# A q stage with one reciprocal for each token tile, and three high-half casts moved from VectorE to ScalarE

## The chip, the cores and the metric

The kernel runs on one core of a Trainium2 chip. The metric is the device time of one execution in microseconds (us). The engines of the core are named as the profile names them: PE (TensorE matmul), PEld (its weight loads), DVE (VectorE), ACT (ScalarE), POOL (GpSimd) and SP (SyncE, which here only issues transfers). Each engine works through its own queue in order: an instruction that waits holds back everything behind it on the same engine.

## What is computed

Random-feature attention over q, k, v (4 batches, 8 heads, 576 tokens, head size 64, 128 features), then a two-matrix layer with a softplus between, then a second layer whose two products are multiplied. All of it is float32:

```python
proj = np.einsum('bhsd,md->bhsm', x, omega)
sq = np.sum(x * x, axis=-1, keepdims=True) / 2.0
h = proj - sq
h = h - np.max(h, axis=-1, keepdims=True)
return np.exp(h) / np.sqrt(m)          # phi
...
q_p, k_p = (phi(q_s), phi(k_s))
kv = np.einsum('bhsm,bhsd->bhmd', k_p, v)
z = np.sum(k_p, axis=2)
num = np.einsum('bhsm,bhmd->bhsd', q_p, kv)
den = np.einsum('bhsm,bhm->bhs', q_p, z)[..., None] + 1e-06
return (num / den).astype(np.float32)
...
g = softplus(x @ w_in);  y = g @ w_out          # first layer
return (((y @ w1) * (y @ w2)) @ w3) @ w_out2    # second layer
```

The change touches the division `num / den`, and the preparation of q for the projection on omega.

## The kernel before

A float32 product is made of three matmuls of operands that were split into a high half (`hi`, rounded) and a low half (`lo` = value minus `hi`): hi*hi, lo*hi, hi*lo (L96). The k stage comes first, then the **q stage**, then the two layers, which use fast (Strassen-like) products with sums of operands (`s1` to `s4`).

The q stage walks over 18 tiles of 128 tokens; a tile has two units of four heads. In turn t of its loop the code emits, in this order: for odd t the numerators of tile t-3; `q_turn` of tile t-2 (eight transposes on PE at L409, whose result ACT copies to `qpt` at L411); `q_feat` of tile t (24 projection matmuls, the maxima `nmax` on DVE at L349, the exponentials on ACT at L354, eight for a tile, half a tile behind); `split_q` of tile t+2 and the next load of q; `x_turn` of tile t-4 (four transposes at L439, the copy `xs` on DVE at L442 or on ACT at L444, and a transfer of it to `xd`); for even t the numerators of tile t-3. `XS_V` lists the tiles whose `xs` DVE copies: 0, 1, 7, 10, 12, 14.

`split_q` makes the halves of q. For tiles 0 to 14 DVE casts the high half (L297, `qt`) and POOL subtracts the low half (L298). Tiles 15, 16 and 17 are split ahead, in turns 9, 10 and 10 (`EARLY`), into slots of the pool `X0` (`qth`, `qtl`); there DVE does both.

`numerators` calls `q_num` for each unit: matmuls against `kv` (a 65th column gives the denominator), then on DVE an add of a small constant (L426, `den`), a reciprocal (L427) and a multiplication into `xt` (L430).

While the q stage still runs, the operands of the first layer's fast product are built from `xd`: loads `xq` on SP (L455, two buffers), casts of high halves on ACT (L469: `xa11h`, `xs1h` and so on), sums `s` (L462) and low halves (L472: `xa11l`, `xs1l` and so on) on DVE. After the last tile comes the layer itself, whose sums of products are made on DVE at L517. A scheduler places every instruction in its engine's queue when the program is built, from its own estimates of durations; a changed instruction can therefore move others too. `FILL` puts the first matmuls of the first layer between the last tiles of the q stage.

Of the kernel before, what the change touches and what calls it, by code (L numbers as in the profile page):

```python
# [19 lines left out]
F32 = mybir.dt.float32  # L20
# [4 lines left out]
ALU = mybir.AluOpType  # L25
AX = mybir.AxisListType

B, H, S, D = 4, 8, 576, 64
M = 128
NT = B * S  # L30
# [41 lines left out]
def body(ctx: ExitStack, tc: tile.TileContext, q, k, k_rest, v, v_rest, om_t, w_in, w_out, w12, w3, wo, out):  # L72
    nc = tc.nc
    cp = ctx.enter_context(tc.tile_pool(name="cp", bufs=1))
    sm = ctx.enter_context(tc.tile_pool(name="sm", bufs=1))
    M_ = ctx.enter_context(tc.tile_pool(name="M_", bufs=14))
# [6 lines left out]
    def ps():  # L83
        return ps_.tile([128, 512], F32, tag="ps", name="ps")
# [10 lines left out]
    def matmul(o, a, b, start, stop, **kw):  # L95
        nc.tensor.matmul(out=o, lhsT=a, rhs=b, start=start, stop=stop, **kw)  # L96
# [177 lines left out]
    def pair(name, bufs):  # L274
        n = small.get(name, (None, 1))[1]
        if n:
            small[name] = sm.tile([128, 2, 4], F32, tag=name, bufs=bufs, name=name), 0
        else:
            small[name] = small[name][0], 1
        return small[name][0][:, 1 - bool(n)]  # L280
# [6 lines left out]
    def xslot(pool, n, dt, name):  # L287
        return pools[pool].tile([128, n], dt, tag="x", name=name)

    kt, vt, kps, kpr, kvs, qts, kacc, raw = {}, {}, {}, {}, {}, {}, {}, {}  # L290
# [2 lines left out]
    def lined(pool, n, **kw):  # L293
        return pool.tile([128, -(-n // LINE) * LINE], F32, **kw)[:, :n]

    def split(hi, lo, f, low=None):
        nc.vector.tensor_copy(out=hi, in_=f)  # L297
        (low or nc.gpsimd).tensor_tensor(out=lo, in0=f, in1=hi.bitcast(F32), op=ALU.subtract)  # L298

    def load_k(i):  # L300
# [8 lines left out]
    def split_k(i):  # L309
        if 0 < i < 2 * B:  # L310
            kt[i] = kt[i - KBUF] if i > KBUF else [K_.tile([128, 2, 512], FR, name=f"kt{i}{x}") for x in "hl"]
            n = 128 if i == 1 else 512
            for o in range(0, 512, n):
                split(*[x[:, :, o:o + n] for x in (*kt[i], raw[i])], nc.gpsimd if i == 1 else nc.vector)
# [12 lines left out]
    def split_q(t):  # L327
        if t >= NT // 128 - len(EARLY):
            free["X0"] -= 2
            qt = [xslot("X0", 512, FR, f"qt{x}") for x in "hl"]  # L330
            split(*qt, raw[t], nc.vector)
        else:
            if len(qbuf) < QBUF:
                qbuf.append(Q_.tile([128, 2, 512], FR, name=f"qt{len(qbuf)}"))
            qt = [qbuf[t % QBUF][:, x, :] for x in range(2)]
            split(*qt, raw[t])
        qts[t] = [x.rearrange("p (c t) -> p c t", c=4) for x in qt]
# [37 lines left out]
    def matmul_half(o, a, b, start, stop):  # L375
        for c in range(0, a.shape[-1], HALF):
            matmul(o[c:c + HALF], a[:, c:c + HALF], b, start, stop, skip_group_check=True)
# [11 lines left out]
        nc.scalar.copy(out=kvs[b][:, 4 * g:4 * g + 4, :], in_=acc)  # L389

    qp, qpt, xt = {}, {}, {}

    def q_feat(u):
        t, g = divmod(u, 2)
        p = project(lambda p: [x[:, 2 * g + p, :] for x in qts[t]])
        if g and t >= NT // 128 - len(EARLY):
            free["X0"] += 2

        def exps():
            qp[u] = M_.tile([128, 4, M], F32, tag="m", name="qp")  # L400
            features(*p, qp[u])

        waiting.append(exps)
        flush(QLAG)
# [5 lines left out]
        qpt[u] = M_.tile([128, 4, 128], F32, tag="m", name="qpt")  # L410
        nc.scalar.copy(out=qpt[u], in_=tp.rearrange("p (h t) -> p h t", h=4))  # L411

    def q_num(u):
        t, g = divmod(u, 2)
        nm = ps()
        nm = nm[:, 0:4 * (D + 1)].rearrange("p (h d) -> p h d", h=4)
        lo, hi = 128 * t, 128 * t + 128
        for h in range(4):
            a = lo
            while a < hi:  # L420
                b = a // S
                e = min(hi, (b + 1) * S)
                matmul_half(nm[a - lo:e - lo, h, :], qpt[u][:, h, a - lo:e - lo], kvs[b][:, 4 * g + h, :], True, True)
                a = e
        den = pair("den", 3)[:, :, None]
        nc.vector.tensor_scalar(out=den, in0=nm[:, :, D:D + 1], scalar1=1e-6 * M, scalar2=None, op0=ALU.add)  # L426
        nc.vector.reciprocal(out=den, in_=den)  # L427
        if g == 0:
            xt[t] = M_.tile([128, H, D], F32, tag="m", name="xt")
        nc.vector.tensor_tensor(  # L430
            out=xt[t][:, 4 * g:4 * g + 4, :], in0=nm[:, :, 0:D],
            in1=den.to_broadcast([128, 4, D]), op=ALU.mult,
        )

    def x_turn(t):
        tp = ps()
# [291 lines left out]
    for i in range(2 * B):  # L728
        if i == B:
            queue += job_ops(win[:1])  # L730
        for t in range(KT):
            k_feat(i, t)
            step(JOB_K)
            if t == 0:
                load_k(i + 4)
            if t == 0 and i >= PRE:
                split_k(i + 2)
            if t == KT - 1 and i:
                kv_sum(i - 1)
                load_v(i + 2)  # L740
            if i == 2 * B - 1 and t < 2:
                split_q(t)
        if i % 4 == 0:
            for g in range(2):
                k_feat_rest(i // 2 + g)
        if i >= 2 * B - 3:
            load_q()
# [3 lines left out]
    nt = NT // 128  # L751
    begun = None

    def fill():
# [3 lines left out]
            x = Up1(0, 0, UP_RATES["Up1"][0])  # L758
            begun = x, x.begin_parts()
        next(begun[1], None)  # L760

    def numerators(t):
        if 0 <= t < nt:
            for g in range(2):
                q_num(2 * t + g)

    for t in range(nt + XLAG):
        if t % 2:
            numerators(t - NLAG)
        for g in range(2):  # L770
            if 0 <= t - TLAG < nt:
                q_turn(2 * (t - TLAG) + g)
        for g in range(2):
            if t < nt:
                q_feat(2 * t + g)
            else:
                flush(0)
            step(JOB_Q[0 in xo])
        for x in [nt - len(EARLY) + n for n, at in enumerate(EARLY) if at == t] + [t + 2] * (t + 2 < nt - len(EARLY)):
            split_q(x)  # L780
            load_q()
        if t == 1:
            kv_sum(2 * B - 1)
            kstack.close()
            pools["X0"] = ctx.enter_context(tc.tile_pool(name="X0", bufs=28, side="right", reuse_waits="tile"))
        if t >= XLAG:
            x_turn(t - XLAG)
            for c in range(2):
                if t - XLAG == 2 * N // 128 * (c + 1) - 1:
                    xo[c], ops = operands(c, xd, "X0")  # L790
                    queue += ops
        if not t % 2:
            numerators(t - NLAG)
        if t in FILL:
            fill()
# [426 lines left out]
```

## Time and profile before

| | |
|---|---|
| median of 3 runs | 811.22 us (810.95 to 811.86) |
| profiled execution | 813.02 us, its span 810.9 us |
| PE busy | 804.0 us, 99% of the span |
| DVE busy | 602.3 us, 74% |
| ACT busy | 441.2 us, 54% |
| q stage in the span | about 51 to 135 us |

The profiled execution is 1.8 us above the median of the runs, and 2.1 us longer than its own span. In a timeline row the first number is the start in us from the start of the span, the second how long it lasted from the first start to the last end, and `x8` the number of instructions in the row; the bracket at its end is the idle time of the engine just before, and what ended it. In a row of a group the numbers are the busy time in us, the mean duration in ns, and the idle time just before the group's instructions.

### The profile page before, as it was taken

Reading aid. Unit: us, or ns where it says so; the run is one execution under the profiler, and the core shown is the slowest. Engines: PE = TensorE matmul, PEld = TensorE weight load, DVE = VectorE, ACT = ScalarE, POOL = GpSimd, SP = SyncE. Lnnn points to the kernel's source line nnn. Section 1 sums busy time; section 2 is a strip of 40 time slices with the busy share of each in tenths; the row PEclk is TensorE's granted clock in tenths of the full one; section 3 lists DMA queues with packets and bytes.
Section 4 is the critical chain, followed back from the end, with each engine's and each line's share of the span. In section 5 each row is a group of like instructions: output and inputs, shape, how many; then the busy total and the mean of one; then the engine's idle time right before and its main releaser. Section 6 shows DMA issues by size and latency. Waiting matters only on the chain.

```text
span 810.9 us, 14465 instructions
## 1 busy us (share of the span) xinstructions
PE 804.0 (99%) x5462; PEld 752.4 (93%) x5462; DVE 602.3 (74%) x1022; ACT 441.2 (54%) x859; POOL 26.5 (3%) x29
## 2 busy tenths in 40 slices
PE   9999999999999999999999999999999999999998
PEld 8999999999999998888888889999999998889998
DVE  6999999878765676754569633897988876888861
ACT  6999998557445676646456432424335123674330
POOL 3033300000000000000000000000000000000000
PEclk9999999999999999999999999999999999999999
DMA  9833635656535558688994642365656556353212
GB/s 288 327 100 87 201 107 172 210 205 214 195 133 195 191 193 259 214 258 293 335 304 148 208 127 79 133 217 186 209 174 214 188 180 237 111 170 122 73 65 78
DMA packets 75861, 150.04 MB, mean 185 GB/s; under 512 B 7184, under 2 KB 44688, under 8 KB 75792
## 3 DMA queue, kind: packets, MB, share of 16 engines
q1 hardware_dynamic: 64016, 101.55, 38.1%
q10 hardware_dynamic: 11776, 47.57, 17.4%
q8 instruction: 43, 0.70, 0.4%
q14 instruction: 26, 0.21, 0.1%
HBM read 98.24 MB, written 50.86 MB: 184 GB/s over the span
## 4 chain that ended last, share of the span: by engine, by line
PE 92%; DVE 4%; DMA 2%; issue 1%; ACT 0%; POOL 0%; ACTq 0%; POOLq 0%
PE ps L96 90%; DMA xq<-xd 1%; PE ps L409 1%; DVE nmax L349 1%; DVE xt L430 1%; DVE s L462 1%; PE ps L439 0%; DVE c L517 0%; DMA rawq<-in_q 0%; DVE u L517 0%; DVE xa22l L472 0%; DVE xa12l L472 0%; DVE qt L297 0%; DVE qtl L298 0%; DVE tlo L191 0%
## 5 line engine op out<-in xcount | busy, mean ns | idle before, releaser
L96 PE MATMUL ps<-dhi,lo 128*128 128x512 f32 x256 | 99.6, 389 | 0.0
L96 PE MATMUL ps<-dlo,hi 128*128 128x512 f32 x256 | 99.6, 389 | 0.0
L96 PE MATMUL ps<-dhi,hi 128*128 128x512 f32 x256 | 99.4, 389 | 0.0
L642 DVE TENSOR_TENSOR dlo<-dn,dhi 128x512 fp32r<-128x512 f32 x64 | 43.8, 689 | 39.1 <-ACT dhi L641 23.0
L517 DVE TENSOR_TENSOR c<-ps,u 128x384 f32<-128x384 f32 x144 | 71.5, 550 | 0.8
L517 DVE TENSOR_TENSOR u<-ps,p 128x384 f32<-128x384 f32 x48 | 26.7, 556 | 53.9 <-PE ps L96 52.3
L524 ACT COPY p<-ps 128x384 f32<-128x384 f32 x48 | 23.0, 480 | 75.8 <-PE ps L96 57.3
L641 ACT CAST dhi<-dn 128x512 fp32r<-128x512 f32 x64 | 39.4, 619 | 45.2 <-DVE dlo L642 25.7
L142 DVE SCALAR_TENSOR_TENSOR f<-raw,f 128x1024 int32<-128x1024 f32 (+2 forms) x43 | 45.5, 1058 | 20.3 <-ACT raw L139 18.8
L557 ACT ACTIVATE c<-c 128x384 f32<-128x384 f32 x72 | 35.1, 524 | 46.8 <-DVE c L517 43.0
L96 PEld LDWEIGHTS ps<-dlo,hi 128*128 128x128 f32 x256 | 48.1, 188 | 10.0
L96 PEld LDWEIGHTS ps<-dhi,hi 128*128 128x128 f32 x256 | 48.1, 188 | 10.0
L96 PEld LDWEIGHTS ps<-dhi,lo 128*128 128x128 f32 x256 | 48.1, 188 | 9.8
L138 ACT ACTIVATE f<-raw,bias 128x1024 f32<-128x1024 int16 (+2 forms) x43 | 46.3, 1084 | 18.9 <-DMA raw<-in_w 9.3
L349 DVE TENSOR_REDUCE nmax<-ps 128x4 f32<-128x512 f32 x72 | 47.0, 683 | 6.2 <-PE ps L96 6.0
L139 ACT ACTIVATE raw<-raw,bias 128x1024 f32<-128x1024 int16 (+2 forms) x43 | 46.3, 1082 | 0.6
L148 DVE SCALAR_TENSOR_TENSOR f<-raw,f 128x1024 int32<-128x1024 int32 (+2 forms) x43 | 45.0, 1046 | 0.6
L354 ACT ACTIVATE qp<-ps,nmax 128x128 f32<-128x128 f32 x144 | 42.2, 457 | 2.4 <-DVE nmax L349 2.4
L354 ACT ACTIVATE kp<-ps,nmax 128x128 f32<-128x128 f32 x128 | 35.5, 460 | 6.0 <-DVE nmax L349 5.9
L96 PE MATMUL ps<-xs1h,thi 128*128 128x384 f32 x96 | 32.4, 337 | 0.2 <-DVE c L517 0.2
L96 PE MATMUL ps<-xs2h,thi 128*128 128x384 f32 x96 | 32.3, 336 | 0.0
L96 PE MATMUL ps<-xs2h,tlo 128*128 128x384 f32 x96 | 32.2, 335 | 0.0
(257 smaller groups left out, 2339.4 us busy)
## 6 DMA issues: line engine op xcount, KB each, us to landing
dn<-gd SPq DMA_DIRECT2D x64, 256.0 KB, 4.0
raw<-in_w ACTq DMA_DIRECT2D x16, 1023.8 KB, 5.8
gd<-c SPq DMA_DIRECT2D x80, 192.0 KB, 2.7
pd<-c SPq DMA_DIRECT2D x48, 192.0 KB, 2.7
raw<-in_w_out ACTq DMA_DIRECT2D x10, 767.8 KB, 4.6
raw<-in_w_in ACTq DMA_DIRECT2D x6, 1023.8 KB, 5.1
rawq<-in_q SPq DMA_DIRECT2D x18, 256.0 KB, 3.1
xd<-xs SPq DMA_DIRECT2D x18, 256.0 KB, 3.3
```

The costliest lines, as they stand in the source:

```text
L96: nc.tensor.matmul(out=o, lhsT=a, rhs=b, start=start, stop=stop, **kw)
L138: nc.scalar.activation(out=self.f, in_=top, func=AF.Relu, scale=TOP, bias=bias[:, 0:1])
L139: nc.scalar.activation(out=self.words(1, F32, 2), in_=top, func=AF.Identity, scale=TOP, bias=bias[:, 1:2])
L142: nc.vector.scalar_tensor_tensor(out=self.f.bitcast(I32), in0=self.words(1, F32, 2), scalar=-2.0 ** 31, in1=self.f, op0=ALU.max, op1=ALU.min)
L148: nc.vector.scalar_tensor_tensor(out=fi, in0=self.words(0, I32, 2), scalar=13, in1=fi, op0=ALU.logical_shift_right, op1=ALU.bitwise_or,)
L349: nc.vector.tensor_reduce(out=nmax, in_=pj, axis=AX.X, op=ALU.max, negate=True)
L354: nc.scalar.activation(out=dst[:, h, :], in_=pj[:, h, :], func=AF.Exp, bias=nmax[:, h:h + 1])
L517: nc.vector.tensor_tensor(out=z, in0=bank, in1=y, op=ALU.add)
L524: nc.scalar.copy(out=p6, in_=b1)
L557: nc.scalar.activation(out=dst, in_=src, func=AF.Softplus)
L641: nc.scalar.copy(out=hi, in_=got[m])
L642: nc.vector.tensor_tensor(out=lo, in0=got.pop(m), in1=hi.bitcast(F32), op=ALU.subtract)
```

## The change

Two things are edited. `split` takes the operation that makes the high half as an argument, and for tiles 15 to 17 that is now a copy on ACT; the low half of these tiles stays on DVE. And `q_num` is folded into `numerators`: the matmuls of both units come first, their two denominators go into one tile of 128 x 2 x 4, one reciprocal of 128 x 8 follows, then the two multiplications. There are 18 reciprocals where there were 36.

```diff
-    def split(hi, lo, f, low=None):
-        nc.vector.tensor_copy(out=hi, in_=f)
+    def split(hi, lo, f, low=None, high=nc.vector.tensor_copy):
+        high(out=hi, in_=f)
         (low or nc.gpsimd).tensor_tensor(out=lo, in0=f, in1=hi.bitcast(F32), op=ALU.subtract)
...
-            split(*qt, raw[t], nc.vector)
+            split(*qt, raw[t], nc.vector, nc.scalar.copy)
...
-    def q_num(u):
-        t, g = divmod(u, 2)
-        nm = ps()
...
-        den = pair("den", 3)[:, :, None]
-        nc.vector.tensor_scalar(out=den, in0=nm[:, :, D:D + 1], scalar1=1e-6 * M, scalar2=None, op0=ALU.add)
+    def numerators(t):
+        if not 0 <= t < nt:
+            return
+        nms = []
...
+        for g in range(2):
+            nm = ps()[:, 0:4 * (D + 1)].rearrange("p (h d) -> p h d", h=4)
...
+            nms.append(nm)
+        den = sm.tile([128, 2, 4, 1], F32, tag="den", bufs=3, name="den")
+        for g in range(2):
+            nc.vector.tensor_scalar(out=den[:, g], in0=nms[g][:, :, D:D + 1], scalar1=1e-6 * M, scalar2=None, op0=ALU.add)
         nc.vector.reciprocal(out=den, in_=den)
...
+        for g in range(2):
+            nc.vector.tensor_tensor(
+                out=xt[t][:, 4 * g:4 * g + 4, :], in0=nms[g][:, :, 0:D],
+                in1=den[:, g].to_broadcast([128, 4, D]), op=ALU.mult,
+            )
```

Line numbers after the edit are higher: the copy `xs` on ACT is L449 (before L444), the cast of an operand L474 (L469), the add of `den` L431 (L426), the reciprocal L432 (L427), the multiplication into `xt` L435 (L430), the sum `s` L467 (L462), the low half of an operand L477 (L472), `qpt` L412 (L411).

The scheduler places other instructions of the q stage anew as well. On ACT, before, in the stretch from about 101 us:

```order
L469 CAST xs3h<-s_1911 128x768
L444 COPY xs<-ps 128x512
L411 COPY qpt<-ps 128x512 x2
L354 ACTIVATE qp<-ps,nmax 128x128 x8
L444 COPY xs<-ps 128x512
L411 COPY qpt<-ps 128x512 x2
L354 ACTIVATE qp<-ps,nmax 128x128 x8
L469 CAST xs1h<-s_2020 128x768
```

In this order two copies `xs` are each followed by the `qpt` of their turn, and the cast `xs1h` comes last. The same stretch of ACT after:

```order
L474 CAST xs3h<-s_1902 128x768
L449 COPY xs<-ps 128x512
L474 CAST xs1h<-s_2009 128x768
L449 COPY xs<-ps 128x512
L412 COPY qpt<-ps 128x512 x2
L354 ACTIVATE qp<-ps,nmax 128x128 x8
L412 COPY qpt<-ps 128x512 x2
L354 ACTIVATE qp<-ps,nmax 128x128 x8
```

The cast `xs1h` and the second copy `xs` now stand ahead of the first copies `qpt`.

On DVE, before, at the end of the q stage, from the last copy `xs` that DVE makes (tile 14) to the last tile's two multiplications into `xt`:

```order
L442 COPY xs<-ps 128x512
L426 TENSOR_SCALAR den<-ps 128x4 x2
...
L472 TENSOR_TENSOR xa11l<-xq,xa11h 128x768
L430 TENSOR_TENSOR xt<-ps,den 128x256
L462 TENSOR_TENSOR s_2539<-xq 128x768
L426 TENSOR_SCALAR den<-ps 128x4
L472 TENSOR_TENSOR xs3l<-s_2492,xs3h 128x768
L427 RECIPROCAL den<-den 128x4
L426 TENSOR_SCALAR den<-ps 128x4
L430 TENSOR_TENSOR xt<-ps,den 128x256
```

In this order the first `xt` of the last tile (the last row) stands behind three operations on operands, `xa11l`, `s_2539` and `xs3l`. The same stretch of DVE after:

```order
L447 COPY xs<-ps 128x512
...
L467 TENSOR_TENSOR s_2475<-xq 128x768
...
L477 TENSOR_TENSOR xa11l<-xq,xa11h 128x768
...
L467 TENSOR_TENSOR s_2521<-xq 128x768
L435 TENSOR_TENSOR xt<-ps,den 128x256 x2
L477 TENSOR_TENSOR xs3l<-s_2475,xs3h 128x768
...
L467 TENSOR_TENSOR s_2524<-s_2521,xq 128x768
...
L477 TENSOR_TENSOR xs1l<-s_2521,xs1h 128x768
L432 RECIPROCAL den<-den 128x8
L477 TENSOR_TENSOR xs2l<-s_2524,xs2h 128x768
L435 TENSOR_TENSOR xt<-ps,den 128x256 x2
```

Now seven operations of 128x768 stand between that copy and the `xt` of the last tile; the first of them, `s_2475`, stood ahead of the copy before, as `s_2492`.

A third move on ACT has one row: the cast `thi` (L187), which stood behind the copies `qpt` of the two turns from 62 us on, stands ahead of them after. The new casts `qth` stand on ACT behind copies `xs`, two together and one by itself.

## Rows read from the trace of the kernel before

**Rows 1.** The page: busy time of the engines, and the chain by engine.

```profile
PE 804.0 (99%) x5462; PEld 752.4 (93%) x5462; DVE 602.3 (74%) x1022; ACT 441.2 (54%) x859; POOL 26.5 (3%) x29
...
PE 92%; DVE 4%; DMA 2%; issue 1%; ACT 0%; POOL 0%; ACTq 0%; POOLq 0%
```

**Rows 2.** Busy time of each engine in stretches of 20 us.

```profile
core 0: us, PE busy (x) PEld busy (x) DVE busy (x) ACT busy (x) POOL busy (x), PEclk, DMA share, GB/s
...
80.00:100.00 20.00, 19.22 (x281) 18.13 (x280) 19.27 (x49) 17.61 (x54) 7.12 (x5) 1.00 0.64 192
100.00:120.00 20.00, 19.20 (x282) 18.14 (x277) 18.82 (x54) 20.00 (x60) 0.00 (x0) 1.00 0.38 116
```

**Rows 3.** Groups of instructions by line and shape, 55 to 140 us.

```profile
L427 DVE RECIPROCAL den<-den 128x4 f32<-128x4 f32 x36 | 5.8, 168 | 0.1
...
L297 DVE CAST qth<-rawq 128x512 fp32r<-128x512 f32 x3 | 2.3, 776 | 1.0 <-DMA rawq<-in_q 1.0
...
L187 ACT CAST thi<-t 128x1024 fp32r<-128x1024 f32 x1 | 1.1, 1150 | 0.0
```

**Rows 4.** The page: the costliest groups, one cast on ACT.

```profile
L641 ACT CAST dhi<-dn 128x512 fp32r<-128x512 f32 x64 | 39.4, 619 | 45.2 <-DVE dlo L642 25.7
```

**Rows 5.** Timeline of PE, 84 to 95 us.

```profile
84.48 0.66 PE L409 MATMUL ps<-ident,qp 128*128 128x128 f32 x4
...
86.58 0.36 PE L96 MATMUL ps<-omh,qt 128*128 128x256 f32 x1 [0.41 <-DVE den L426]
...
93.37 1.09 PE L409 MATMUL ps<-ident,qp 128*128 128x128 f32 x8
94.22 0.36 PE L96 MATMUL ps<-omh,qt 128*128 128x256 f32 x1
```

**Rows 6.** Timelines of DVE and POOL, 81 to 88 us.

```profile
82.11 1.50 DVE L297 CAST qth<-rawq 128x512 fp32r<-128x512 f32 x1
...
86.35 0.17 DVE L427 RECIPROCAL den<-den 128x4 f32<-128x4 f32 x1
86.43 0.13 DVE L426 TENSOR_SCALAR den<-ps 128x4 f32<-128x4 f32 x1
...
87.52 0.40 DVE L297 CAST qth<-rawq 128x512 fp32r<-128x512 f32 x1
...
81.73 1.60 POOL L298 TENSOR_TENSOR qt<-rawq,qt 128x512 fp32r<-128x512 f32 x1 [2.89 <-DVE qt L297]
```

**Rows 7.** Timeline of PE, 101 to 104 us.

```profile
101.00 0.66 PE L409 MATMUL ps<-ident,qp 128*128 128x128 f32 x4
...
103.11 0.39 PE L96 MATMUL ps<-omh,qt 128*128 128x256 f32 x1 [0.55 <-ACT xs L444]
```

**Rows 8.** Timeline of ACT, 101 to 104 us.

```profile
101.68 0.90 ACT L469 CAST xs3h<-s 128x768 fp32r<-128x768 f32 x1
102.40 0.66 ACT L444 COPY xs<-ps 128x512 f32<-128x512 f32 x1
102.88 1.16 ACT L411 COPY qpt<-ps 128x512 f32<-128x512 f32 x2
```

**Rows 9.** Timeline of DVE at the end of the q stage.

```profile
123.63 0.95 DVE L472 TENSOR_TENSOR xs4l<-s,xs4h 128x768 fp32r<-128x768 f32 x1
124.50 0.68 DVE L442 COPY xs<-ps 128x512 f32<-128x512 f32 x1
125.10 0.22 DVE L426 TENSOR_SCALAR den<-ps 128x4 f32<-128x4 f32 x2
...
128.70 0.96 DVE L462 TENSOR_TENSOR s<-xq 128x768 f32<-128x768 f32 x1 [0.64 <-DMA xq<-xd]
...
130.72 0.42 DVE L430 TENSOR_TENSOR xt<-ps,den 128x256 f32<-128x256 f32 x1
```

**Rows 10.** Timeline of PE: the last tile's `xt` turned, and a later wait.

```profile
131.29 0.41 PE L439 MATMUL ps<-ident,xt 128*128 128x128 f32 x2 [0.28 <-DVE den L427]
...
149.89 0.44 PE L96 MATMUL ps<-xs1h,thi 128*128 128x384 f32 x1 [0.24 <-DVE c L517]
```

**Rows 11.** The chain of waits in order of time, 140 to 148 us.

```profile
140.84 7.08 DMA xq<-xd
...
147.94 0.96 DVE s L462
```

More of the change, by code (lines that the diff above doesn't have):

```diff
@@ L391, in body @@
     qp, qpt, xt = {}, {}, {}
+    nt = NT // 128
     def q_feat(u):
@@ L411, in q_turn @@
         nc.scalar.copy(out=qpt[u], in_=tp.rearrange("p (h t) -> p h t", h=4))
-    def q_num(u):
-        t, g = divmod(u, 2)
-        nm = ps()
-        nm = nm[:, 0:4 * (D + 1)].rearrange("p (h d) -> p h d", h=4)
+    def numerators(t):
+        if not 0 <= t < nt:
+            return
+        nms = []
         lo, hi = 128 * t, 128 * t + 128
[L418 to L424, printed above, removed]
-        den = pair("den", 3)[:, :, None]
-        nc.vector.tensor_scalar(out=den, in0=nm[:, :, D:D + 1], scalar1=1e-6 * M, scalar2=None, op0=ALU.add)
-        nc.vector.reciprocal(out=den, in_=den)
[L428 to L433, printed above, removed]
+        for g in range(2):
+            nm = ps()[:, 0:4 * (D + 1)].rearrange("p (h d) -> p h d", h=4)
+            for h in range(4):
+                a = lo
+                while a < hi:
+                    b = a // S
+                    e = min(hi, (b + 1) * S)
+                    matmul_half(nm[a - lo:e - lo, h, :], qpt[2 * t + g][:, h, a - lo:e - lo], kvs[b][:, 4 * g + h, :], True, True)
+                    a = e
+            nms.append(nm)
+        den = sm.tile([128, 2, 4, 1], F32, tag="den", bufs=3, name="den")
+        for g in range(2):
+            nc.vector.tensor_scalar(out=den[:, g], in0=nms[g][:, :, D:D + 1], scalar1=1e-6 * M, scalar2=None, op0=ALU.add)
+        nc.vector.reciprocal(out=den, in_=den)
+        xt[t] = M_.tile([128, H, D], F32, tag="m", name="xt")
+        for g in range(2):
[3 more added lines that the diff above has]
+            )
     def x_turn(t):
@@ L760, in fill @@
         next(begun[1], None)
[L762 to L765, printed above, removed]
     for t in range(nt + XLAG):
```

## The prediction

> **What bounds the kernel now.** I read the busy times first: PE works 99% of the span, and 92% of the chain of waits is PE [rows 1]. What other engines do counts only where PE waits for them. DVE and ACT are nearly as full as PE where the change acts: of 20 us, DVE is busy 19.27 and then 18.82, ACT 17.61 and then 20.00 [rows 2]. So work taken from DVE can help there, and work given to ACT lands on an engine without room. PE's granted clock is 1.00 in these stretches, its upper level (2.4 GHz) [rows 2], so nothing is to be had from that.
>
> Next I looked in PE's timeline for the places in the q stage where it loses time. Undisturbed, the eight transposes of a turn start 0.85 us before the first projection (93.37 to 94.22) [rows 5]. At 84.48 it is 2.10 us (to 86.58): 1.25 us lost, behind DVE. At 101.00 it is 2.11 us (to 103.11): 1.26 us lost, behind ACT [rows 7]. At the end of the stage PE waits 0.28 us for the last tile's `xt`, and at 149.89 it waits 0.24 us for a DVE sum [rows 10]. Together about 3.0 us. A change that only relieves DVE and ACT in this stage can win no more than that.
>
> **The work itself.** Eighteen reciprocals go. One has a mean duration of 168 ns [rows 3], but the next DVE instruction starts 0.08 us after it (86.35 to 86.43) [rows 6], so DVE gains 18 x 0.08 = 1.4 us at the least and 18 x 0.168 = 3.0 at the most; I take the start-to-start value, since DVE's queue is full. A reciprocal over 8 columns has no row; it lies between one and two of 4 columns, 0.08 to 0.17 us, so the upper end costs back up to all of the gain, and the lower end none. I take the lower: a multiplication of 256 columns takes 0.42 us [rows 9] where a reciprocal of four takes 0.17, so four columns more are worth little.
>
> Three casts leave DVE: 2.3 us [rows 3]. Two of them are some 0.4 us (87.52) and one took 1.50 us, at 82.11, while POOL ran a subtraction from 81.73 for 1.60 us [rows 6]. The casts' wait of 1.0 us for a load of q [rows 3] leaves DVE too. On ACT no cast of this shape has run in this stage; the nearest row is a cast of the same shape in a later stage, 619 ns [rows 4]. Start to start, ACT's copy `xs` of 128x512 takes 0.48 us (102.40 to 102.88) [rows 8]. So ACT gets 3 x 0.48 to 3 x 0.62, 1.4 to 1.9 us; I take 1.4, since ACT's queue is full there too. All of this lies beside PE and costs or brings nothing by itself. The first `xt` of a tile now waits for the second unit's numerators; its transposes come a turn later, so that is covered, but for the last tile, where the order below costs more.
>
> The Trainium skill, page "SBUF — State Buffer", section "Who interferes with whom", says that a DVE cast in a fast mode and a GpSimd operation take turns on a shared pair of ports, one blocked until the other ends; the 1.50 us cast beside the POOL subtraction agrees. By that rule alone the change would win the 1.1 us by which that cast is longer than its sister, since ScalarE has ports of its own: 810.1 us. It speaks for the rival "relief" below.
>
> **Where PE's waits go.**
>
> 1. *84 us.* Here DVE is late by the 1.50 us cast. With the cast on ACT, and the load's wait gone from DVE, DVE is more than 1.25 us earlier. I take the whole: -1.25 us. The next thing due is the exponentials on ACT, which now hold the added casts behind a copy `xs`; at 0.48 us each they would give back at most 0.96 here.
>
> 2. *62 us.* The cast `thi` now stands ahead of two turns of `qpt` on ACT. It takes 1.15 us [rows 3]; PE has no such loss there now, so the cost is between 0 and 1.15. I take the middle, +0.5.
>
> 3. *101 us.* Now `xs3h` (0.72 us, 101.68 to 102.40) and one `xs` (0.48) stand ahead of `qpt` on ACT [rows 8], and PE loses 1.26 there. After, `xs1h` and another `xs` stand there as well: 1.2 us more. The loss then lies between 1.26, if ACT comes earlier by what it saved in waiting, and 2.46, if nothing is saved. PE comes earlier by step 1 and so meets ACT no better. I take 2.0 (a part before, a part after the first projections of this turn): +0.75 against before.
>
> The three sum to -1.25 + 0.5 + 0.75 = 0.0.
>
> 4. *The end of the q stage.* PE turns the last tile's `xt` at 131.29 and already waits for it [rows 10]; so each delay of this `xt` is a delay of PE. On DVE, one operation of 128x768 takes 0.87 us from start to start (123.63 to 124.50) [rows 9]. Before, from the copy `xs` at 124.50 to this `xt` at 130.72, three such operations stand, and a wait of 0.64 us for a load. After, seven stand there. One of them was ahead of the copy, which brings the copy forward by 0.87. So: -0.87 + 4 x 0.87 - 0.64 (the load is issued when its buffer is free, which is earlier) - 2 x 0.08 (reciprocals) = +1.8 us. The matmuls that can run before that are in their old places, so PE has nothing to put into the gap. If the load still holds DVE up, it is +2.4; if DVE comes to the copy earlier by the 1.4 us of reciprocals, +0.4.
>
> 5. *149.89.* The DVE sum that PE waits for stood behind a sum that waited for a load issued at 140.84, 7.08 us long [rows 11]. After, the order of SP puts both such loads together and ahead of the stores that stood between them, so the wait should be gone: -0.24.
>
> Sum: 0.0 + 1.8 - 0.24 = +1.6 us. The profiled execution would go from a span of 810.9 to 812.5 us and from 813.02 to 814.6; the median of the runs, 1.8 us lower, from 811.22 to **812.8**.
>
> **The rivals.** *Balance*: DVE comes early to the end of the stage, +0.4 for step 4, and the steps before give nothing: +0.2 or 811.4. For it speaks that both savings lie on DVE ahead of that place; against it, that DVE must wait for the maxima of PE's last projections there, which cannot come earlier than PE.
>
> *Relief*: the waits behind DVE and ACT go and nothing takes their place. Then -1.25 - 1.26 - 0.28 - 0.24 = -3.0, 808.2. For it speaks that DVE is 94 to 96% full in this stage; against it, that ACT is as full [rows 2] and that the orders put more ahead of `qpt` and `xt`, not less. The Trainium skill, page "Perfetto Trace Analysis", section "Optimizing Scalar/DVE Operations", says that work may be given to Scalar when DVE is saturated; the trace has DVE saturated, and Scalar too.
>
> *ACT is the bound*: slower. The casts (1.9 us at the row of 619 ns), `thi` (1.15) and step 3's upper end (+1.2) all reach PE, with step 4 as above: -1.25 + 1.15 + 1.2 + 1.8 and half of the casts, 0.9, make +3.8, 815.0. It decides where ACT has no idle time left from 82 us to the end of the stage, and 100 to 120 us is such a stretch already. Against it: 2.4 us of idle in the other [rows 2].
>
> That the change doesn't do what it says, I exclude: the orders show 18 reciprocals and three casts on ACT.
>
> **How the numbers follow.** About 0.2%, 1.6 us, is what a measurement of this kernel can tell from no change; the bounds are 809.6 and 812.84. My forecast (step 4 as worked out, the rest balanced) has a chance of 0.48 with a range of its own of 811.6 to 814.0; it lies on the bound, so half of it is "same" and half "slower". Balance has 0.20, all "same". Relief has 0.18, "faster". ACT as the bound has 0.14, "slower". So faster 0.18, same 0.24 + 0.20 = 0.44, slower 0.24 + 0.14 = 0.38. The range leaves out about half of relief and half of the slowest case: 809.0 to 814.8.
>
> **What would show it.** In the timeline of PE after: no gap at 84 us behind DVE's `den` (step 1); a gap of about 2 us in all near 101 to 107 us whose releaser is ACT (step 3); above all a gap of 1.5 to 2.2 us before the two transposes of the last tile's `xt`, whose releaser is DVE, with the seven operations ahead of it (step 4); none behind the DVE sum at about 150 us (step 5). If the last tile's `xt` comes before its transposes are due, the forecast is wrong and the time is 811 or less. If the gap at 84 us stays, the cast was not its cause.

## The result and the profile after

The changed kernel takes 816.19 us (median of six runs, 815.33 to 817.02), the kernel before 811.69 in six runs beside it: a ratio of 1.0056, 95% interval 1.0043 to 1.0069. It is 4.5 us **slower**, where the forecast was 1.6 us and the range ended at 814.8. The span of the profiled execution went from 810.9 to 814.9 us.

The page of the kernel after, its busy times and the chain by engine (compare [rows 1]):

```profile
PE 802.9 (99%) x5462; PEld 751.6 (92%) x5462; DVE 600.1 (74%) x1001; ACT 443.6 (54%) x862; POOL 26.1 (3%) x29
...
PE 89%; ACT 7%; DVE 2%; DMA 1%; issue 1%; ACTq 0%; SPq 0%; DVEq 0%
```

DVE lost 21 instructions and 2.2 us of work, ACT gained three and 2.4 us. That is what the edit says, and it moved PE's own work by nothing. But ACT, 0% of the chain before, is now 7%: PE has begun to wait for it. The windows of 20 us say where (compare [rows 2]):

```profile
core 0: us, PE busy (x) PEld busy (x) DVE busy (x) ACT busy (x) POOL busy (x), PEclk, DMA share, GB/s
80.00:100.00 20.00, 19.91 (x276) 18.83 (x276) 16.86 (x42) 18.72 (x57) 6.41 (x5) 1.00 0.56 177
100.00:120.00 20.00, 17.48 (x270) 15.95 (x268) 18.76 (x44) 18.52 (x55) 0.00 (x0) 1.00 0.29 84
120.00:140.00 20.00, 17.59 (x203) 15.85 (x198) 17.91 (x39) 16.97 (x38) 0.00 (x0) 1.00 0.53 160
```

From 80 to 100 us PE gained (19.22 to 19.91 us busy) and DVE was relieved (19.27 to 16.86). From 100 to 120 us PE fell from 19.20 to 17.48, although ACT fell too, from 20.00 to 18.52: two engines idle at once, each for the other. From 120 to 140 us it lost again.

The same account as a table: the start of the same PE instruction in both timelines, and how far the kernel after is behind.

| PE instruction | before, us | after, us | behind |
|---|---|---|---|
| transposes of `qp`, 57 us | 56.95 | 57.16 | 0.2 |
| transposes of `qp`, 61 us | 61.20 | 62.22 | 1.0 |
| transposes of `xt`, 66 us | 66.27 | 67.80 | 1.5 |
| transposes ahead of the gap at 84 us [rows 5] | 84.48 | 85.93 | 1.4 |
| transposes one turn later | 88.52 | 88.73 | 0.2 |
| transposes of `qp`, 96 us | 96.17 | 96.61 | 0.4 |
| transposes of `xt`, 107 us | 107.38 | 110.07 | 2.7 |
| transposes of `xt`, 121 us | 121.31 | 123.97 | 2.7 |
| the last tile's `xt` [rows 10] | 131.29 | 136.29 | 5.0 |
| the wait at 150 us [rows 10] | 149.89 | 154.50 | 4.6 |
| end of the span | 810.9 | 814.9 | 4.0 |

A trace is one execution. Up to 59 us every queue holds the same order in all thirteen traces of this study, and still the other twelve lie between 0.1 and 1.5 us behind the kernel before at 61 us. So the 1.0 us that the kernel after is behind there is no effect of the change. It came with a load of k; DVE at about 22 us, the first row before, the second after:

```profile
21.05 0.69 DVE L297 CAST kt1h<-rawk 128x1024 fp32r<-128x1024 f32 x1
...
22.07 0.69 DVE L297 CAST kt1h<-rawk 128x1024 fp32r<-128x1024 f32 x1 [1.11 <-DMA rawk<-in_k]
```

DVE waited 1.11 us for that load, ACT was 1.0 us late from 25 us on, and PE met that at 58 us, where it lost 0.8 us. Why the load came later stays open.

**At 84 us.** PE's timeline after; the answer to [rows 5]:

```profile
85.93 1.09 PE L410 MATMUL ps<-ident,qp 128*128 128x128 f32 x8
86.78 0.36 PE L96 MATMUL ps<-omh,qt 128*128 128x256 f32 x1
```

The transposes and the first projection are 0.85 us apart, undisturbed; the 1.25 us are gone.

**From 101 us.** PE after; the answer to [rows 7]:

```profile
101.84 0.66 PE L410 MATMUL ps<-ident,qp 128*128 128x128 f32 x4 [0.33 <-ACT qp L354]
102.87 0.65 PE L410 MATMUL ps<-ident,qp 128*128 128x128 f32 x4 [0.38 <-ACT qp L354]
...
104.08 0.39 PE L96 MATMUL ps<-omh,qt 128*128 128x256 f32 x1 [0.55 <-ACT xs L449]
...
105.61 0.60 PE L444 MATMUL ps<-ident,xt 128*128 128x128 f32 x4
106.88 0.66 PE L410 MATMUL ps<-ident,qp 128*128 128x128 f32 x4 [0.68 <-ACT xs L449]
108.13 0.33 PE L410 MATMUL ps<-ident,qp 128*128 128x128 f32 x1 [0.59 <-ACT qp L354]
```

and ACT in the same stretch; the answer to [rows 8]:

```profile
102.64 0.90 ACT L474 CAST xs3h<-s 128x768 fp32r<-128x768 f32 x1
103.36 0.67 ACT L449 COPY xs<-ps 128x512 f32<-128x512 f32 x1
103.84 0.92 ACT L474 CAST xs1h<-s 128x768 fp32r<-128x768 f32 x1
106.24 0.59 ACT L449 COPY xs<-ps 128x512 f32<-128x512 f32 x1 [1.49 <-PE ps L444]
106.73 1.08 ACT L412 COPY qpt<-ps 128x512 f32<-128x512 f32 x2
```

These rows are to be read together. The projections at 104.08 wait for the first `xs` copy to free its bank. ACT, done with `xs1h`, has the second `xs` next in its queue, and its source is the transposes L444 at 105.61, which PE makes only after those same projections. So ACT stands idle for 1.49 us with the copies `qpt` ready behind it, and then PE stands idle, at 106.88 and 108.13, since `qpt` and the exponentials behind it are late.

**The end of the q stage.** PE after; the answer to [rows 10]:

```profile
131.32 0.41 PE L444 MATMUL ps<-ident,xt 128*128 128x128 f32 x2 [0.81 <-ACT qpt L412]
...
136.29 0.44 PE L444 MATMUL ps<-ident,xt 128*128 128x128 f32 x2 [1.60 <-DVE xt L435]
```

and DVE; the answer to [rows 9]:

```profile
126.37 0.68 DVE L447 COPY xs<-ps 128x512 f32<-128x512 f32 x1
...
133.00 0.16 DVE L431 TENSOR_SCALAR den<-ps 128x4 f32<-128x4 f32 x1 [0.64 <-PE ps L96]
133.08 0.95 DVE L467 TENSOR_TENSOR s<-s,xq 128x768 f32<-128x768 f32 x1
133.94 0.16 DVE L431 TENSOR_SCALAR den<-ps 128x4 f32<-128x4 f32 x1
134.02 0.95 DVE L477 TENSOR_TENSOR xs1l<-s,xs1h 128x768 fp32r<-128x768 f32 x1
134.88 0.20 DVE L432 RECIPROCAL den<-den 128x8 f32<-128x8 f32 x1
134.99 0.91 DVE L477 TENSOR_TENSOR xs2l<-s,xs2h 128x768 fp32r<-128x768 f32 x1
135.82 0.75 DVE L435 TENSOR_TENSOR xt<-ps,den 128x256 f32<-128x256 f32 x2
```

From the copy to the last `xt` it is 9.45 us, 6.22 before (124.50 to 130.72). Both numerators were there at 133.94; three operations of 128x768 ran between the first of them and the `xt` on which PE waited.

### The profile page after: what moved, and what is told of

Same layout as the page of the kernel before. It is cut to its first block, busy times and chain, and to the rows that moved or that the text cites. A ratio compares the mean times of both kernels' runs of the same rounds, so it can differ in the third digit from the quotient of the medians.

```text
span 814.9 us, 14449 instructions
## 1 busy us (share of the span) xinstructions
PE 802.9 (99%) x5462; PEld 751.6 (92%) x5462; DVE 600.1 (74%) x1001; ACT 443.6 (54%) x862; POOL 26.1 (3%) x29
## 4 chain that ended last, share of the span: by engine, by line
PE 89%; ACT 7%; DVE 2%; DMA 1%; issue 1%; ACTq 0%; SPq 0%; DVEq 0%
PE ps L96 87%; ACT qp L354 2%; ACT kp L354 2%; ACT qpt L412 1%; PE ps L410 1%; PE ps L444 1%; DMA xq<-xd 1%; DMA rawk<-in_k 0%; DMA xd<-xs 0%; DVE nmax L349 0%; ACT f L138 0%; ACT raw L139 0%; ACT xs L449 0%; ACT thi L187 0%; DVE xs1l L477 0%
## 5 line engine op out<-in xcount | busy, mean ns | idle before, releaser
L187 ACT CAST thi<-t 128x1024 fp32r<-128x1024 f32 x16 | 17.2, 1074 | 28.0 <-PE ps L96 22.8
```

## The experiments

Three theories stood against each other. *Order*: the loss comes from where the scheduler puts other work, once there is one reciprocal. *ACT load*: the three casts make ACT late. *Pairing*: every `xt` waits for the numerators of both units. In the second set, "too little slack" was the rival: the queues are so full that moving one thing only makes another late. All ratios below are to the kernel before, run beside it.

**Each part alone.** The merge with the casts left on DVE:

```diff
-            split(*qt, raw[t], nc.vector, nc.scalar.copy)
+            split(*qt, raw[t], nc.vector)
```

> One reciprocal for both units, the three casts stay on DVE. ACT's order is that of the changed kernel without its three casts. Theory 'order' (the loss comes from where the scheduler puts other work once there is one reciprocal): 3 to 5 us slower than before, with the waits at about 101 to 108 us and before the last tile's xt still there. Theory 'ACT load' (the three casts make ACT late): within 1 us of before. Theory 'pairing' (each xt waits for both units' numerators): slower too, 1 to 4 us.

817.95 us, ratio 1.0065 (1.0048 to 1.0081): 5.3 us slower. PE's waits at the two places are there again, and two more came at 80 us (0.72 and 0.61 us), where DVE still has the casts and stands 1.49 us with one of them, until a load of q lands:

```profile
79.57 0.43 DVE L297 CAST qth<-rawq 128x512 fp32r<-128x512 f32 x1 [1.49 <-DMA rawq<-in_q]
...
80.47 0.36 PE L96 MATMUL ps<-omh,qt 128*128 128x256 f32 x1 [0.72 <-DVE xt L435]
...
109.38 0.66 PE L410 MATMUL ps<-ident,qp 128*128 128x128 f32 x4 [0.68 <-ACT xs L449]
110.62 0.33 PE L410 MATMUL ps<-ident,qp 128*128 128x128 f32 x1 [0.59 <-ACT qp L354]
...
139.39 0.44 PE L444 MATMUL ps<-ident,xt 128*128 128x128 f32 x2 [1.62 <-DVE xt L435]
```

So the whole loss is there without one added instruction on ACT, though part of it lies elsewhere: from 78 to 82 us PE loses 1.7 us here, 0.3 in the kernel after. The other part, with one reciprocal for each unit as before (against the kernel before):

```diff
-            split(*qt, raw[t], nc.vector)
+            split(*qt, raw[t], nc.vector, nc.scalar.copy)
```

> The three casts go to ACT, each unit keeps its reciprocal. Theory 'order': no loss, 0 to 1.5 us faster than before, because the wait at 84 us goes and the order at 101 us and at the end of the stage is that of before. Theory 'ACT load': 2 to 5 us slower. Theory 'pairing': as before.

812.88 us, ratio 1.0000 (0.9990 to 1.0011): no change. The gap at 84 us is gone in its trace as well (transposes at 86.22, first projection at 87.07, 0.85 us apart), a gain of 1.2 us. Of that 0.8 us is lost at 74 us, where PE waits for exponentials on ACT; another 0.8 is lost at 58 us, where no order differs yet. "ACT load" has fallen: what the three casts on ACT save and what they cost is together nothing that can be measured. "Faster by 0 to 1.5 us" was the expectation of "order", and its lower end came.

**The pairing without the merge.** The changed kernel's form, with two reciprocals for a tile, and the casts on DVE:

```diff
-        nc.vector.reciprocal(out=den, in_=den)
+        for g in range(2):
+            nc.vector.reciprocal(out=den[:, g], in_=den[:, g])
...
-            split(*qt, raw[t], nc.vector, nc.scalar.copy)
+            split(*qt, raw[t], nc.vector)
```

> The code form of the changed kernel (matmuls of both units, then the divisions of both), but with two reciprocals for a tile, and the casts on DVE. The scheduler's order at 62 us and at the end of the stage is then close to that of before; at 101 us the cast xs1h stands ahead of qpt, the second xs does not. Theory 'order': within 1.5 us of before. Theory 'pairing': as slow as the merge alone. Theory 'ACT load': as before.

814.15 us, ratio 1.0024 (1.0014 to 1.0033), 1.9 us slower. All three theories missed: it is outside the "within 1.5 us" of "order" (though the interval begins at 1.1 us), far from the 5.3 us of the merge, and not "as before". Its trace has one wait that the pairing explains:

```profile
133.24 0.44 PE L445 MATMUL ps<-ident,xt 128*128 128x128 f32 x2 [1.40 <-DVE xt L436]
```

Here the last tile's first `xt` stands behind both units' numerators and one operation of 128x768 more than before. From 98 to 121 us, where the merge loses 3, this kernel loses nothing. So the pairing costs part of the loss at the end of the stage, and the rest comes with the missing reciprocal: by the order that it leads to, as the edges below bear out.

**A priority for the numerators.** The changed kernel, with the numerators traced at a higher priority:

```diff
         if t % 2:
-            numerators(t - NLAG)
+            with tc.high_priority(URGENT):
+                numerators(t - NLAG)
```

(and the same for even t)

> The changed kernel whole, but the numerators have a higher scheduling priority, so that at 101 us qpt stands ahead of xs1h and of the second xs, at the end of the stage the last qpt stands ahead of xs, and one operation less stands ahead of the last tile's xt. Theory 'order': the waits at 101 to 108 us shrink by about 2 us and those at the end by 1 us or more, 1 us slower to 1 us faster than before. Theories 'ACT load' and 'pairing': no better than the changed kernel, 3 to 5 us slower than before.

815.74 us, ratio 1.0039 (1.0025 to 1.0054): 3.2 us slower. That is a miss for "order" as I had put it, and lies where "ACT load" and "pairing" had put it. The loss from 96 to 107 us did shrink, from 2.3 to 0.9 us. But a priority moves much else too:

```profile
80.37 0.39 PE L96 MATMUL ps<-omh,qt 128*128 128x256 f32 x1 [1.48 <-ACT xs L449]
...
135.35 0.44 PE L444 MATMUL ps<-ident,xt 128*128 128x128 f32 x2 [1.33 <-DVE xt L435]
```

A wait of 1.48 us stands at 80 us where there was none, and the one at the end, six operations instead of seven, hardly changed. So this run does not separate the three. After this the orders were set one at a time, by an edge between two instructions of one queue, which adds no wait for data.

**One place: ACT.** The changed kernel; each copy `xs` on ACT is queued behind the last `qpt` emitted before it:

```diff
-            nc.scalar.copy(out=xs, in_=tp.rearrange("p (c t) -> p c t", c=KD))
+            with tc.issue_after(turned[-1]):
+                nc.scalar.copy(out=xs, in_=tp.rearrange("p (c t) -> p c t", c=KD))
```

> The changed kernel whole; only on ACT each copy xs is queued behind the copies qpt emitted before it, so at 101 us the second xs stands behind qpt, and at the end of the stage the last qpt stands ahead of xs. Theory 'order': PE's waits at 104 to 109 us lose about 1.6 us of their 3.4, the wait of 0.98 us for the last qpt goes, one operation less stands before the last tile's xt; together about 3 us faster than the changed kernel, 0.5 to 2 us slower than before. Rival 'too little slack' (the queues are full, and whatever is moved makes something else late): no more than 1 us faster than the changed kernel.

814.80 us, ratio 1.0028 (1.0015 to 1.0041). That is 0.28% or 2.3 us less than the changed kernel's 1.0056; about 3 were expected, and 0.5 to 2 us above the kernel before, where it is 2.3. From 96 to 107 us PE loses 0.4 us, 2.3 in the changed kernel. The waits at 106.88 and 108.13 and the one at 131.32 are gone, and of PE's waits from 100 us on these stay:

```profile
102.71 0.66 PE L411 MATMUL ps<-ident,qp 128*128 128x128 f32 x4 [0.35 <-ACT qp L354]
103.92 0.39 PE L96 MATMUL ps<-omh,qt 128*128 128x256 f32 x1 [0.55 <-ACT xs L451]
133.64 0.44 PE L445 MATMUL ps<-ident,xt 128*128 128x128 f32 x2 [1.79 <-DVE xt L436]
```

The first two are the loss that the kernel before has there as well [rows 7].

**One place: DVE.** The changed kernel; `s2`, `xs1l` and `xs2l` of the second block are queued behind the last tile's `xt`:

```diff
+    def behind(i):
+        tc.add_manual_dep(i, ended[0].name, mybir.DependencyInfo(
+            mybir.DependencyClass.NoSync, mybir.DependencyReason.DATA), reason="last xt first")
...
+                if src is xd and c == 1 and name in ("s1", "s2"):
+                    hold(i)
```

> The changed kernel whole; only on DVE the sum s2 and the low halves xs1l and xs2l of the second block are queued behind the last tile's xt, so that four operations of 128x768 stand before it, not seven. Theory 'order': the wait of 1.76 us before the last tile's transposes shrinks to 0.3 us or less, all else stays: 1.4 to 1.8 us faster than the changed kernel, 2 to 3.5 us slower than before. Rival 'too little slack': the three operations come late for the matmuls on them, and the time is that of the changed kernel within 0.7 us.

814.76 us, ratio 1.0027 (1.0016 to 1.0038), 2.3 us less than the changed kernel, where 1.4 to 1.8 were expected. The wait before the last tile's transposes is gone; the wait for the last `qpt` (0.81 us at 130.02) stays, as it should.

**Both places.**

> The changed kernel with both orders set as in the two runs beside it. Theory 'order': the two gains add up, 4 to 5 us faster than the changed kernel, so within 1 us of before. Rival 'too little slack': 2 us faster than the changed kernel at most.

812.83 us, ratio 1.0000 (0.9991 to 1.0008). The two gains add up: 0.28 + 0.29 is 0.57%, all that the change had cost. Its waits from 100 us on:

```profile
103.15 0.66 PE L422 MATMUL ps<-ident,qp 128*128 128x128 f32 x4 [0.38 <-ACT qp L354]
104.35 0.39 PE L96 MATMUL ps<-omh,qt 128*128 128x256 f32 x1 [0.55 <-ACT xs L466]
132.56 0.44 PE L460 MATMUL ps<-ident,xt 128*128 128x128 f32 x2 [0.29 <-DVE xt L447]
```

They answer [rows 7] and [rows 10] almost to the number. So "order" is shown: with the reciprocal merged, the units paired and the casts on ACT, two orders decide the 4.5 us.

**Can the relief be had?** With both places set, three more kernels queue casts on ACT behind `qpt`. First all of them, the operands' (L469 before) and `thi`:

> As both_places, and on ACT the casts of operands' high halves and the casts thi of transposed weights are queued behind the qpt emitted before them too. Theory 'order': the waits at 57 to 66 us (about 1.3 us in the changed kernel) shrink by 0.5 us or more, and the rest of the wait at 101 us goes: 0 to 2.5 us faster than before. Rival 'too little slack': no better than both_places, or slower since the casts come late for DVE.

814.91 us, ratio 1.0025 (1.0015 to 1.0036), 2.0 us slower than before: "order" missed, and the rival had the time right. PE's waits went to DVE:

```profile
100.14 1.27 POOL L300 TENSOR_TENSOR qt<-rawq,qt 128x512 fp32r<-128x512 f32 x1 [8.48 <-PE ps L96]
...
100.30 1.93 DVE L486 TENSOR_TENSOR s<-xq 128x768 f32<-128x768 f32 x1
...
102.70 0.36 PE L96 MATMUL ps<-omh,qt 128*128 128x256 f32 x1 [1.44 <-DVE xt L449]
...
129.39 0.96 DVE L486 TENSOR_TENSOR s<-xq 128x768 f32<-128x768 f32 x1 [1.49 <-DMA xq<-xd]
...
132.97 0.44 PE L462 MATMUL ps<-ident,xt 128*128 128x128 f32 x2 [1.87 <-DVE xt L449]
```

The rival's reason, that the casts come late for DVE, is not in these rows: from 95 to 135 us DVE waits for no cast on ACT. The `xt` that PE waited for at 102.70 stood behind a sum that took 1.93 us beside a subtraction on POOL, in place of 0.95, and the one at 132.97 behind a wait of 1.49 us for a load. Whether the later casts made that load late isn't shown.

Then `thi` alone, and `thi` with the one cast `xs1h`:

```diff
-            nc.scalar.copy(out=self.thi, in_=self.t)
+            i = nc.scalar.copy(out=self.thi, in_=self.t).ins
+            if turned and len(turned) < 10:
+                tc.add_manual_dep(i, turned[-1].name, ..., reason="turn first")
```

> As both_places, and of the casts on ACT only thi (transposed weights) is queued behind the qpt emitted before it. Theory 'order': the waits at 57 to 66 us (0.86 us from before in both_places) shrink by 0.5 us or more and the rest stays, 0.2 to 1.5 us faster than before. Rival 'too little slack': thi comes late for DVE and what waits for it, and the time is that of both_places or longer.

> As both_places_and_thi, and the one cast xs1h of the first block is queued behind the qpt emitted before it, so that on ACT the order at 101 us is that of the kernel before. Theory 'order': no more than 0.7 us from both_places_and_thi either way, since both_places lost nothing to xs1h by its trace (its loss at 103 us is behind xs3h and xs). Rival 'too little slack': DVE, which needs xs1h, comes late with xt, as in both_places_and_casts, and the time is 1 us or more above both_places_and_thi.

812.40 us, ratio 1.0003 (0.9994 to 1.0012), and 812.91 us, 1.0007 (0.9997 to 1.0016). The two are alike, as "order" expected for `xs1h`. But the gain of `thi` isn't there. Its wait did go: from 61 to 66 us this kernel lost nothing, both_places 0.5 us. But from 57 to 61 us it lost 0.8, both_places 0.3, where no order differs yet. At 101 us PE was 1.1 us ahead of the kernel before, and at 105 us it was 0.1 behind. The rows of POOL, DVE and PE of the first of the two say why:

```profile
100.32 1.27 POOL L300 TENSOR_TENSOR qt<-rawq,qt 128x512 fp32r<-128x512 f32 x1 [8.61 <-PE ps L96]
...
100.48 1.93 DVE L486 TENSOR_TENSOR s<-xq 128x768 f32<-128x768 f32 x1
...
102.88 0.36 PE L96 MATMUL ps<-omh,qt 128*128 128x256 f32 x1 [1.47 <-DVE xt L449]
```

The cast of q tile 14 on DVE had moved to 99.77, POOL's subtraction followed it at 100.32, and the sum on DVE, 0.95 us elsewhere, took 1.93: it ended 0.82 us after the subtraction did. It is the same meeting as in the kernel with all casts. So that cast was put back:

```diff
+            if x == 14:
+                with tc.high_priority(URGENT):
+                    split_q(x)
```

> As both_places_and_thi, and the split of q tile 14 has a higher scheduling priority, so that on DVE its cast stands before the copy xs again, not after xa11l, and POOL's subtraction of that tile ends before the sum s1 of the first block starts. In both_places_and_thi that sum took 1.93 us beside the subtraction, where it takes 0.95 alone, and PE waited 1.6 us for the xt behind it. Theory 'order', with the collision as the cause of what was given back at 103 us: that sum takes 0.95 us, the waits at 101 to 105 us shrink by 0.5 to 1.0 us, and the time is 0.3 to 1.5 us below before. Rival 'too little slack': the wait passes to xs and qpt on ACT, and the time is that of both_places_and_thi within 0.4 us.

811.95 us, ratio 0.9992 (0.9983 to 1.0001). POOL's subtraction is at 96.42 and the same sum takes 0.91 us:

```profile
101.06 0.91 DVE L486 TENSOR_TENSOR s<-xq 128x768 f32<-128x768 f32 x1
```

From 98 to 107 us PE loses 0.4 us, 1.2 in the kernel with `thi` alone, and the profiled span, one execution, is 809.5 us, 1.4 below before. The sign is as expected, and it is the fastest kernel of the study, but the interval touches no change, so a gain over the kernel before isn't shown; nor is one over the kernel with `thi` alone, since their intervals overlap.

## Why the prediction was wrong

The direction of the worked sum was right, though the chances had "same" (0.44) ahead of "slower" (0.38). Two of its five places came as they were written, and a third in kind. It failed in size: +1.6 us against +4.5, and the upper end of the range lay under the result.

1. *84 us, -1.25.* Right: -1.2 us (1.4 behind to 0.2). The casts on DVE were the cause, since the gap goes with the casts alone too. Nor did it go because PE came later: with `thi` queued behind `qpt`, PE makes these transposes at 84.59, 0.1 us behind, and the first projection at 85.44. That it was the cast of 1.50 us, and not the others or the load's wait, was not tested by itself; and 0.37 us of PE's waits there before had ACT as releaser (85.51), which I had put down to DVE.
2. *62 us, +0.5 for `thi`.* Right, with some luck, since it was the middle of a range from 0 to 1.15: the table shows +1.2 from 57 to 84 us, but 0.8 of it is at 58 us. What is left is 0.5 from 61 to 66 us, which goes when `thi` is queued behind `qpt`. The 0.8 at 58 us came with the load of k.
3. *101 us, +0.75.* **This term failed**: +2.3 us (0.4 to 2.7 behind). I bounded it by durations: what is put ahead of `qpt` costs at most what it takes, 1.2 us. But an instruction ahead in a queue costs its wait as well, and the second `xs` waited 1.49 us for transposes that PE makes after the work it was itself held up in. With `xs` queued behind `qpt` PE lost 0.4 there. The upper end of 2.46 for the whole loss was no bound; it measured 3.5 (1.26 and 2.25).
4. *The end, +1.8.* The mechanism was right (seven operations ahead of the last `xt`, a wait of 1.60 us with DVE as its releaser), the size too small: +2.3. Left out was the wait of 0.81 us for the last `qpt`, which ACT copies after an `xs` now. It made the numerators late, so DVE waited 0.64 us at 133.00; both waits go when `xs` is queued behind `qpt`. The order of ACT that showed it I had read at 101 us only.
5. *150 us, -0.24.* Right in kind: the wait is gone, and PE gains 0.5 us there. But it is gone with the casts alone too, where SP keeps the two loads apart as before, so the cause that I gave isn't shown. Another 0.5 us comes back from 158 to 203 us; what gives it isn't shown.

The sum of the profile is 0.2 + 1.2 - 1.2 + 0.2 + 2.3 + 0.0 + 2.3 - 1.0 = 4.0, the difference of the spans. That is 2.4 us more than the forecast: steps 3 and 4 with 2.0, the time up to 61 us with 1.0 and 88 to 96 us with 0.2, less 0.8 at 150 us and behind it. Without the time up to 61 us the two traces differ by 3.0 us, the medians by 4.5; where the other 1.5 us lie isn't shown.

Of the rivals, "ACT is the bound" came nearest with 815.0, yet not by its reason: the casts, to which it gave 0.9 us, cost nothing alone, and in the changed order no cost of them shows either (1.0056 with them, 1.0065 without, and these intervals overlap). "Balance" failed since DVE's saving of reciprocals does not reach the end of the stage: DVE waits there for PE's numerators. "Relief" failed as the orders said it would.

The prices of single instructions were close. Reciprocal and cast in the kernel after (compare [rows 3, 4]):

```profile
L432 DVE RECIPROCAL den<-den 128x8 f32<-128x8 f32 x18 | 3.6, 201 | 0.3
...
L297 ACT CAST qth<-rawq 128x512 fp32r<-128x512 f32 x3 | 2.6, 853 | 0.5 <-DMA rawq<-in_q 0.5
```

Eight columns take 201 ns where four took 168; the cast takes 853 ns, but after the one that stands by itself the next instruction starts 0.52 us later (86.84 to 87.36), within the 0.48 to 0.62 that I gave it. The wait for a load of q went with the casts: ACT now waits 0.5 us for it.

## What to carry to other kernels

When a scheduler sets the queues, the price of an edit is in the instructions that it moves, not in those that it saves: compare the orders on each engine, and do it at every place where the bounding engine has little slack. An instruction that comes ahead in a queue costs its duration and also the wait for its source; look whether that source stands, on another engine, behind the very work that is being held up. To tell such a cause from the edit itself, put back one order at a time with an edge inside one queue; a change of priority for all numerators moved too much to tell anything.

## What the runs showed of the hardware

A subtraction on POOL held up work on DVE in two places, and each time the DVE instruction ended after POOL's: a cast of 0.40 us took 1.50 [rows 6], and a sum of two SBUF tiles took 1.93 us in place of 0.91, in three kernels alike (1.92 to 1.93). The Trainium skill, page "SBUF — State Buffer", section "Who interferes with whom", says that a DVE instruction with two SBUF inputs contends with a GpSimd instruction that reads SBUF, and that the later one waits for the other's end; the second case agrees: the sum started 0.16 us after the subtraction and ended 0.82 us after it, nearly its own time alone. What I had not expected is that such a meeting can come from nothing but a moved order: with it PE lost 1.2 us from 98 to 107 us, without it 0.4. These are single traces; in the times of the two kernels (1.0003 and 0.9992) that difference is not clear of noise.
